# Routing attention: the centroid products moved behind the sums of weights, with the choice, the codes, the division and the row writes moved after them

## The chip, the cores and the metric

The kernel runs on one core of a Trainium2 chip. The metric is the device time of one execution in microseconds (us). Three runs of the kernel before took 707.80, 705.94 and 705.63 us, with a median of 705.94. A profile records one execution, instruction by instruction, with the engines PE (TensorE: matmuls), DVE (VectorE), ACT (ScalarE), POOL (GpSimd) and SP (SyncE, which here only issues DMAs).

## The reference

Two blocks follow each other. The first is attention in which a query sees only keys of its own cluster; the second sends each token to one of eight experts.

```python
# attention: B=4, H=8, S=768, D=64, 16 clusters a head
q_assign = np.argmax(np.einsum('bhsd,hcd->bhsc', q_n, c_n), axis=-1)   # q, k, centroids divided
k_assign = np.argmax(np.einsum('bhsd,hcd->bhsc', k_n, c_n), axis=-1)   # by their norms
mask = q_assign[:, :, :, None] == k_assign[:, :, None, :]
scores = np.where(mask, scale * np.matmul(q, k.transpose(0, 1, 3, 2)), -1000000000.0)
attn = np.exp(scores - np.max(scores, axis=-1, keepdims=True))
attn = attn / (np.sum(attn, axis=-1, keepdims=True) + 1e-09)
x = np.matmul(attn, v)            # then (B,H,S,D) -> (B*S, H*D) = (3072, 512)
# experts: E=8, 512 -> 1024 -> 512
expert_idx = np.argmax(xn @ en.T / tau, axis=1)
out[mask] = gate_w[mask, None] * (np.maximum(x[mask] @ w1[e], 0.0) @ w2[e])
```

## The kernel before

Attention goes by pairs of heads: 16 pairs (`n`), four to a batch (`nb` = 0 to 3 in batch `b`). A pair has twelve units, that is two halves of the queries times six blocks of 128 keys, and is worked in six turns (`it` = 0 to 5) of two units each. In a turn the code writes, in this order: the scores and the exponents of the two units that come next (so turn 5 computes scores of the next pair), then `between(n, it)`, then `attend` for this turn's two units, then some work that is named by the turn. Every engine runs its instructions in the order in which this code writes them; nothing reorders them later.

A unit's scores (L484) are four short matmuls on `hot` (bf16), which add a large negative number where clusters differ, and four float matmuls of queries and keys, all on quarters of the array (64*64). ACT takes the exponent (`expo`, L495) into one of five buffers `prob`. `attend` multiplies with the values (L506, 64*64 as well), and DVE adds the exponents up in `acc` (L515 for the first two units of a half, L525 for the others). At the end of a half (turns 2 and 5), ACT copies the result out (`o_sb`, L530) and POOL joins its two parts (`unite`, L539).

The mask of the next pair is prepared during a pair, in steps:
- `turn0` and `turn1` (L386) turn the queries and keys of the pair after next, on DVE, in turns 4 and 5.
- `products` (L396): PE multiplies queries and keys with the centroids, on column strips of the array (128*32), into a bank of `misc`; DVE brings it out (`asn`, L405). Turn 0, ahead of `attend`.
- `choose`: four DVE operations (L414 to L417) find the chosen cluster; three ACT operations (L419, L422) write the codes `cd`; then SP issues a transposing DMA (L427) that makes `hot` of them. Turn 1.
- `hot` is first used by the scores of turn 5.

The result of the pair before is finished in the same pair:
- `total`: PE sums `acc` over the keys (L553, 128*32, into a bank of `misc`), DVE turns the sums and inverts them (L570, L571), POOL spreads the inverses (L574). Turn 0, after `attend`.
- `divide`: DVE makes `den` (L585) and `xT` (L589). Turn 2, after `attend`.
- `rows`: DVE turns `xT` into rows `xb` (L606) and SP writes them to `x_rows` with four DMAs (L613). Turn 3.

There are two `misc` banks, handed out in turn. In the first pair of each later batch the products for the routing of the batch before (L632, 128*32) stand in turn 4; from pair 10 on, small hooks for the early experts (`ranks`, L768, `firsts`, `dest`, `hot_rows`, `tokens`, L950) are put between the turns. SP's other DMAs come from the same code: v of the next pair in turn 2 (L195), q and k of a later pair in turns 4 and 5 (L208), reads of `x_rows` (L654) and, from pair 11, expert weights (L1091). After the last pair the experts' stage takes the rest of the time; it is not touched.

Of the kernel before, what the change touches and what calls it, by code (L numbers as in the profile page):

```python
# [39 lines left out]
def kernel(  # L40
# [140 lines left out]
    NP = len(pairs)  # L181
# [43 lines left out]
    def keep_up(n):  # L225

        for _ in range(n):
            nc.tensor.matmul(
                idle_ps[:, 0].rearrange("p (g x) -> p g x", x=P),
                lhsT=onesb,  # L230
                rhs=bc(onesb, [P, 4, P], 1),
                start=True,
                stop=True,
            )
# [88 lines left out]
    def begin():  # L323

        nc.scalar.dma_start(out=c_sb, in_=centroids.rearrange("h c d -> (h c) d"))
        load(0, "q")
        load(0, "k")
        load(0, "v")
        load(1, "qk")
        constants()  # L330

        nc.scalar.activation(en_r, epsc[0:E], ACTF.Sqrt)
        nc.scalar.dma_start(out=emb, in_=moe_expert_emb)
        nc.scalar.dma_start(out=tau, in_=moe_tau.to_broadcast([E, 1]))
        norm_rows(cn_r, c_sb, P)
        unit_centroids()
        keep_up(2)
        piece(0, "turn0")
        piece(0, "turn1")
        norm_rows(en_r, emb, E)  # L340

        nc.scalar.activation(cn_r, epsc, ACTF.Exp)
        piece(0, "products")
        for m in range(2):
            scores(m, (1,))
        piece(0, "choose")
        keep_up(6)
        piece(0, "turn_numbers")
        for m in range(2):
            scores(m, (0,))  # L350
            expo(m)
        token_numbers()
        unit_experts()

    def prep_pieces(n):

        hp = pairs[n][1]
        t = ld[n]

        def in_halves(kT):  # L360

            return kT.rearrange("p (s i t) -> p i s t", i=2, t=SQ)

        def turn(nm, half):
            if half == 0:
                t[nm + "T"] = trp.tile([P, S], F32, tag=nm + "T", name=nm + "T")
            bk = misc()
            for j in range(NJ // 2):
                nc.tensor.transpose(
                    bk[:, P * j : P * j + P],  # L370
                    t[nm][:, NJ // 2 * half + j].rearrange("p h d -> p (h d)"),
                    ident,
                )
            if nm == "q":
                nc.scalar.copy(t["qT"][:, HS * half : HS * half + HS], bk[:, 0:HS])
            else:
                nc.vector.tensor_copy(
                    in_halves(t["kT"])[:, half], bk[:, 0:HS].rearrange("p (s t) -> p s t", t=SQ)
                )

        def turn_blocks(nm):
            t[nm + "T"] = trp.tile([P, S], F32, tag=nm + "T", name=nm + "T")
            dst, src = t[nm + "T"], t[nm].rearrange("p j h d -> p (j h d)")
            if nm == "k":
                dst, src = in_halves(dst), src.rearrange("p (i s t) -> p i s t", i=2, t=SQ)
            nc.vector.transpose(dst, src)  # L386

        def products():

            bk = misc()  # L390
            for i in range(4):
                if i < 2:
                    r = t["qT"][:, HS * i : HS * i + HS]
                else:
                    r = in_halves(t["kT"])[:, i - 2]
                nc.tensor.matmul(  # L396
                    bk[2 * C * i : 2 * C * i + 2 * C, 0:HS],
                    lhsT=cnB[:, hp],
                    rhs=r,
                    start=True,  # L400
                    stop=True,
                )

            t["asn"] = smp.tile([P, HS], F32, tag="asn", name="asn", bufs=1)
            nc.vector.transpose(t["asn"], bk[:, 0:HS])  # L405

        def choose():

            shp = [P, S // SQ, C]
            asn = t["asn"].rearrange("p (g c) -> p g c", c=C)  # L410
            amax = smp.tile(shp[0:2], F32, tag="amax", name="amax")
            sel = smp.tile(shp, BF16, tag="sel", name="sel", bufs=1)
            pm = smp.tile(shp[0:2], BF16, tag="pm", name="pm")
            nc.vector.tensor_reduce(amax, asn, axis=AXX, op=ALU.max)  # L414
            nc.vector.tensor_tensor(sel, asn, bc(amax, shp, 2), ALU.is_equal)
            nc.vector.tensor_tensor(sel, sel, bc(prefc, shp, 1), ALU.mult)
            nc.vector.tensor_reduce(pm, sel, axis=AXX, op=ALU.max)  # L417
            pm = pm.rearrange("p (s h) -> p s h", h=2)
            nc.scalar.activation(cd[..., 1], pm, ACTF.Copy, scale=wcd)  # L419
            for i, p0 in enumerate((0, D)):  # L420
                g = slice(p0, p0 + D)
                nc.scalar.activation(  # L422
                    cd[g, :, :, 2 * i], pm[g], ACTF.Square, scale=(BIG**0.5, 1.0)[i]
                )
            t["H"] = trp.tile([P, S // (2 * SQ), P], BF16, tag="hot", name="hot")
            if n > 0:
                nc.sync.dma_start_transpose(  # L427
                    out=t["H"], in_=cd.rearrange("p s h c -> p (s h c)")
                )

        def turn_numbers():

            U = S // (4 * SQ)
            for half in range(2):
                bk = misc().bitcast(BF16)
                for u in range(U):
                    nc.tensor.transpose(
                        bk[:, P * u : P * u + P],
                        cd[:, U * half + u].rearrange("p h c -> p (h c)"),
                        identb,  # L440
                    )
                bk = bk[:, 0 : P * U].rearrange("r (s x) -> r s x", x=P)
                ss = slice(U * half, U * half + U)
                nc.scalar.copy(t["H"][:, ss, D:], bk[:, :, D:])
                nc.vector.tensor_copy(t["H"][:, ss, 0:D], bk[:, :, 0:D])

        return {
            "turn0": lambda: turn_blocks("q") if n else (turn("q", 0), turn("k", 0)),
            "turn1": lambda: turn_blocks("k") if n else (turn("q", 1), turn("k", 1)),
            "products": products,  # L450
            "choose": choose,
            "turn_numbers": turn_numbers,
        }

# [840 lines left out]
    prepare, route = {}, {}  # L1295
# [30 lines left out]
    def piece(n, name, *args):  # L1326
        if n < NP:
            if n not in prepare:
                prepare[n] = prep_pieces(n)
            prepare[n][name](*args)  # L1330

    def between(n, it):
        b, nb = divmod(n, NHP)
        if n == 0:

            if it == 0:
                piece(1, "turn0")
                piece(1, "turn1")
            elif it == 1:
                piece(1, "products")  # L1340
            elif it == 2:
                piece(1, "choose")
                turned_experts()
            elif it == 3:
                later_constants()
        elif it == 0:
            piece(n + 1, "products")
        elif it == 1:
            piece(n + 1, "choose")
        elif it == 3:  # L1350
            rows(2 * n - 2, 2 * n - 1)
        if it == 4:
            piece(n + 2, "turn0")
# [2 lines left out]
        if b > 0:  # L1356
            if nb == 0 and it == 3:
                route[b - 1] = route_pieces(b - 1)
            products, logits, read, norms, choose = route.get(b - 1, (None,) * 5)


            m = NJ * nb + it
            if m in (8, 11, 14):
                read((m - 8) // 3 * 2, (m - 8) // 3 * 2 + 2)
            if m in (15, 16, 18, 19, 21, 22):
                norms((15, 16, 18, 19, 21, 22).index(m))
            if (nb, it) == (0, 4):
                products(0, 1)
            elif (nb, it) == (0, 5):
                logits(0, 1)  # L1370
            elif (nb, it) == (1, 4):
                choose()
# [29 lines left out]
    with tc.manual_schedule(engines=by_hand):  # L1402
        begin()
        for i in range(0, len(units), 2):
# [8 lines left out]
            for m in range(i + 2, min(i + 4, len(units))):  # L1413
                scores(m)
                expo(m)
            between(n, it)
            if it == 4 and n == NP - 1:
                divide(2 * n)
# [8 lines left out]
            for m in range(i, i + 2):  # L1427
                attend(m)
            if it == 2:
                if n > 0:  # L1430
                    divide(2 * n - 2, 2 * n - 1)
                unite(2 * n)
            elif it == 5:
                unite(2 * n + 1)
            if i + 2 == len(units):
# [1 line left out]
                route[b][0](0)  # L1437
            if it == 0 and n > 0:
                total(2 * n - 2, 2 * n - 1)
            elif it == 3 and n == NP - 1:  # L1440
                total(2 * n)
        at.close()
        mop = ctx.enter_context(tc.tile_pool(name="mop", bufs=2, **tile_waits))
# [196 lines left out]
```

## Time and profile before

| what | value |
|---|---|
| median of three runs | 705.94 us |
| the profiled execution: its own time | 709.17 us |
| its span, first to last instruction | 707.4 us |
| granted TensorE clock, mean | 0.996 |
| PE busy | 692.3 us |
| DVE busy | 382.0 us |
| ACT busy | 264.5 us |
| POOL busy | 263.0 us |
| scores on `hot` (L484), 768 matmuls | 65.5 us, 329 ns each |
| float scores (L484), 1536 matmuls | 156.8 us, 484 ns each |
| values' products (L506), 1536 matmuls | 142.0 us, 486 ns each |
| centroid products (L396), 128 matmuls | 498 ns each |
| sums of weights (L553), 248 matmuls | 15.9 us, 338 ns each |
| exponents (L495), 192 | 153.5 us, 811 ns each |

A float matmul stands as two instructions, and the four quarters or strips of the array work at once, so the means are not a rate. Matmuls are pipelined and their ends are modelled; the start of an instruction is the surer number. In the lines below, "x8" means that eight instructions of one kind are shown as one, the first number is the start in us from the span's start, and a bracket gives the engine's idle time before it and what ended it. Waits of SP are not shown as idle time.

### The profile page before, as it was taken

How to read it: one execution, taken by the hardware profiler on the slowest of the kernel's cores; microseconds unless marked ns; L12 is line 12 of the kernel's file. 1: busy time of each engine (PE TensorE's matmuls, PEld its weight loads, DVE VectorE, ACT ScalarE, POOL GpSimd, SP SyncE). 2: the span in 40 equal slices, each digit the busy share in tenths (PEclk: the TensorE clock that was granted, in tenths of full speed). 3: DMA queues.
4: the chain of work that ended last, by engine and by line, in shares of the span. 5: the costliest groups of instructions: out<-in, count | busy, mean ns of one | idle time of the engine just before them, and what ended most of it. 6: DMA issues, size and time to landing. Idle time of an engine off the chain costs nothing.

```text
span 707.4 us, 16123 instructions
## 1 busy us (share of the span) xinstructions
PE 692.3 (98%) x6518; PEld 455.4 (64%) x6518; DVE 382.0 (54%) x665; ACT 264.5 (37%) x446; POOL 263.0 (37%) x402
## 2 busy tenths in 40 slices
PE   7999999999999999999999999999999999999997
PEld 3444444444444444454966668897979797979694
DVE  4688888998889999998583121240220303030310
ACT  4566655577566655676315110101010111111111
POOL 2122221322224221454224446656264454635403
PEclk9999999999999999999999999999999999999999
DMA  9546656776657787779799977268758486869360
GB/s 148 84 65 105 105 99 100 139 158 114 100 92 158 125 147 157 158 188 331 172 317 347 333 281 271 71 241 288 258 211 305 183 312 220 313 228 341 123 247 31
DMA packets 244123, 135.54 MB, mean 192 GB/s; under 512 B 207808, under 2 KB 207810, under 8 KB 244044
## 3 DMA queue, kind: packets, MB, share of 16 engines
q1 hardware_dynamic: 237852, 121.28, 63.8%
q0 software_dynamic: 6016, 13.12, 5.3%
q8 instruction: 54, 0.88, 0.5%
q14 instruction: 25, 0.20, 0.1%
q10 hardware_dynamic: 176, 0.05, 0.0%
HBM read 115.92 MB, written 13.12 MB: 182 GB/s over the span
## 4 chain that ended last, share of the span: by engine, by line
PE 80%; DVE 6%; issue 5%; DMA 5%; another core or an unknown queue 1%; ACT 1%; POOL 1%; SPq 1%; POOLq 0%; DVEq 0%; ACTq 0%
PE s_ps L484 19%; PE o_ps L506 15%; PE h_ps L1261 10%; PE y_ps L1277 9%; PE h_ps L1176 9%; PE y_ps L1213 5%; PE misc L1213 5%; PE x_ps L1176 3%; DMA out_dram<-ys,spidx 3%; DVE acc L525 2%; PE misc L553 2%; PE misc L396 2%; DMA x_rows<-xb 1%; PE misc L632 1%
## 5 line engine op out<-in xcount | busy, mean ns | idle before, releaser
L495 ACT ACTIVATE prob<-s_ps 128x768 f32<-128x768 f32 x192 | 153.5, 811 | 97.1 <-PE s_ps L484 83.4
L484 PE MATMUL s_ps<-qT,kT 64*64 64x384 f32 x1536 | 156.8, 484 | 0.0
L506 PE MATMUL o_ps<-prob,v 64*64 64x385 f32 x1536 | 142.0, 486 | 0.0
L525 DVE TENSOR_TENSOR acc<-acc,prob 128x768 f32<-128x768 f32 x128 | 125.7, 982 | 8.8 <-ACT cd L422 0.5
L506 PEld LDWEIGHTS o_ps<-prob,v 64*64 64x64 f32 x1536 | 54.7, 133 | 70.2 <-issue 58.4
L1222 DVE STREAM_TRANSPOSE ys<-y_ps 128x256 f32<-128x256 f32 (+4 forms) x16 | 6.6, 414 | 155.4 <-PE y_ps L1213 138.7
L1261 PE MATMUL h_ps<-xTm,w1s 128*128 128x128 f32 x768 | 88.6, 275 | 1.4 <-issue 1.4
L1261 PEld LDWEIGHTS h_ps<-xTm,w1s 128*128 128x128 f32 x768 | 87.6, 192 | 3.0 <-issue 2.6
L1277 PE MATMUL y_ps<-w2s,hT 128*128 128x512 f32 x192 | 85.3, 594 | 1.7 <-ACT hT L1268 1.0
L539 POOL TENSOR_TENSOR o_sum<-o_sb 128x385 f32<-128x385 f32 x30 | 31.4, 1048 | 148.1 <-ACT o_sb L530 148.1
L1052 POOL DMA_INDIRECT out_dram<-ys,spidx x56 | 56.9, 1017 | 74.1 <-DVE ys L1236 59.4
L484 PEld LDWEIGHTS s_ps<-qT,kT 64*64 64x64 f32 x1536 | 56.4, 134 | 38.5 <-issue 35.3
L1268 ACT ACTIVATE hT<-h_ps 128x512 f32<-128x512 f32 x24 | 14.3, 596 | 162.9 <-PE h_ps L1261 119.1
L1176 PE MATMUL h_ps<-xTs,w1s 128*128 128x272 f32 (+7 forms) x384 | 72.9, 346 | 1.1 <-ACTq L1537 1.1
L1176 PEld LDWEIGHTS h_ps<-xTs,w1s 128*128 128x128 f32 x384 | 66.6, 190 | 8.0 <-issue 2.4
L484 PE MATMUL s_ps<-hot 64*64 64x384 bf16 x768 | 65.5, 329 | 2.4 <-ACT prob L495 1.3
L574 POOL COPY inv<-inv 32x12 f32<-32x12 f32 x120 | 42.9, 358 | 55.2 <-DVE inv L571 50.8
L1277 PEld LDWEIGHTS y_ps<-w2s,hT 128*128 128x128 f32 x192 | 35.3, 190 | 42.9 <-issue 40.2
L1041 POOL DMA_INDIRECT xs<-x_rows,gpidx x56 | 56.4, 1007 | 17.1 <-issue 16.5
L484 PEld LDWEIGHTS <-hot 64*64 64x64 bf16 x768 | 23.7, 107 | 40.3 <-issue 39.1
L1213 PE MATMUL y_ps<-hTs,w2o 128*128 128x272 f32 (+7 forms) x256 | 48.0, 346 | 0.0
L1213 PE MATMUL misc<-hTs,w2o 128*128 128x272 f32 (+7 forms) x256 | 48.0, 346 | 0.0
(264 smaller groups left out, 680.0 us busy)
## 6 DMA issues: line engine op xcount, KB each, us to landing
w1s<-in_moe_w_dram SPq DMA_DIRECT2D x18, 2048.0 KB
w2s<-in_moe_w_dram SPq DMA_DIRECT2D x18, 2048.0 KB
v<-in_v_dram SPq DMA_DIRECT2D x128, 48.0 KB
q<-in_q_dram SPq DMA_DIRECT2D x60, 96.0 KB
k<-in_k_dram SPq DMA_DIRECT2D x60, 96.0 KB
x_rows<-xb SPq DMA_DIRECT2D x60, 96.0 KB
xr<-x_rows SPq DMA_DIRECT2D x9, 512.0 KB
w1s<-in_moe_w_dram SPq DMA_DIRECT2D x4, 1024.0 KB
```

Source lines behind the costliest of these rows:

```text
L484: nc.tensor.matmul(s_ps[D * half : D * half + D, h, 0:HS], lhsT=l[rows, half], rhs=r[rows], start=part == (1 if len(parts) < 2 else 0), st ...
L495: nc.scalar.activation(d["prob"][:, :, 0:HS], d["s_ps"][:, :, 0:HS], ACTF.Exp, scale=scale)
L506: nc.tensor.matmul(g["o_ps"][D * h : D * h + D, half, 0:HE], lhsT=ld[n]["v"][keys, j, h], rhs=d["prob"][keys, h, 0:HE], start=(j == 0), st ...
L525: nc.vector.tensor_tensor(g["acc"], g["acc"], d["prob"][:, :, 0:HS], ALU.add)
L539: add(t["o_sum"][:, hq], t["o_sb"][:, 0], t["o_sb"][:, 1], ALU.add)
L574: nc.gpsimd.tensor_copy(inv2[M * to : M * to + M, :, i % 2], inv[M * i : M * i + M])
L1041: nc.gpsimd.indirect_dma_start(out=to, out_offset=None, in_=of, in_offset=bass.IndirectOffsetOnAxis(ap=at, axis=0), bounds_check=n - 1, oo ...
L1052: inst = nc.gpsimd.indirect_dma_start(out=to, out_offset=bass.IndirectOffsetOnAxis(ap=at, axis=0), in_=of, in_offset=None, bounds_check=n - 1,
L1176: nc.tensor.matmul(bk, lhsT=w1s[it.slot][:, c, P * f : P * f + P], rhs=d["xT"][:, c, 0:C], start=(c == 0), stop=(c == KD - 1),)
L1213: nc.tensor.matmul(bks[g][:, 0:C], lhsT=d["w2"][:, f, P * g : P * g + P], rhs=d["hT"][:, f, 0:C], start=(f == 0), stop=(f == KF - 1),)
L1261: nc.tensor.matmul(bk[:, m : m + P], lhsT=w1s[it.slot][:, c, f0 + m : f0 + m + P], rhs=d["xT"][:, P * c : P * c + P], start=(c == 0), stop ...
L1277: nc.tensor.matmul(bk, lhsT=d["hT"][:, P * c : P * c + P], rhs=w2s[it.slot][:, c], start=(c == 0), stop=(c == KF - 1),)
```

## The change

Six pieces of work are written at other places:
- `products` goes from ahead of `attend` in turn 0 to behind `total`, which is behind `attend`. (In pair 0, which has no `total`, it stays in turn 1 but goes behind `attend`.)
- `choose` goes from turn 1 to turn 2. It is cut in two: its ACT operations and the transposing DMA become `codes`, which ACT runs in turn 3, between the exponents of that turn's two units.
- `divide` goes from turn 2 to turn 3.
- `rows` goes from turn 3 to turn 0 of the following pair; the last ones are written in turn 4 of pair 15.
- The routing products of a finished batch stay in turn 4 but go behind `attend`.

No operation is added or left out.

```diff
@@ -344,6 +344,7 @@
         for m in range(2):
             scores(m, (1,))
         piece(0, "choose")
+        piece(0, "codes")
         keep_up(6)
         piece(0, "turn_numbers")
         for m in range(2):
@@ -415,7 +416,10 @@
             nc.vector.tensor_tensor(sel, asn, bc(amax, shp, 2), ALU.is_equal)
             nc.vector.tensor_tensor(sel, sel, bc(prefc, shp, 1), ALU.mult)
             nc.vector.tensor_reduce(pm, sel, axis=AXX, op=ALU.max)
-            pm = pm.rearrange("p (s h) -> p s h", h=2)
+            t["pm"] = pm.rearrange("p (s h) -> p s h", h=2)
+
+        def codes():
+            pm = t["pm"]
             nc.scalar.activation(cd[..., 1], pm, ACTF.Copy, scale=wcd)
             for i, p0 in enumerate((0, D)):
                 g = slice(p0, p0 + D)
@@ -449,6 +453,7 @@
             "turn1": lambda: turn_blocks("k") if n else (turn("q", 1), turn("k", 1)),
             "products": products,
             "choose": choose,
+            "codes": codes,
             "turn_numbers": turn_numbers,
         }
 
@@ -1336,18 +1341,16 @@
             if it == 0:
                 piece(1, "turn0")
                 piece(1, "turn1")
-            elif it == 1:
-                piece(1, "products")
             elif it == 2:
                 piece(1, "choose")
                 turned_experts()
             elif it == 3:
                 later_constants()
-        elif it == 0:
-            piece(n + 1, "products")
-        elif it == 1:
+        elif it == 0 and n > 1:
+            rows(2 * n - 4, 2 * n - 3)
+        elif it == 2:
             piece(n + 1, "choose")
-        elif it == 3:
+        elif it == 4 and n == NP - 1:
             rows(2 * n - 2, 2 * n - 1)
         if it == 4:
             piece(n + 2, "turn0")
@@ -1364,9 +1367,7 @@
                 read((m - 8) // 3 * 2, (m - 8) // 3 * 2 + 2)
             if m in (15, 16, 18, 19, 21, 22):
                 norms((15, 16, 18, 19, 21, 22).index(m))
-            if (nb, it) == (0, 4):
-                products(0, 1)
-            elif (nb, it) == (0, 5):
+            if (nb, it) == (0, 5):
                 logits(0, 1)
             elif (nb, it) == (1, 4):
                 choose()
@@ -1413,6 +1414,8 @@
             for m in range(i + 2, min(i + 4, len(units))):
                 scores(m)
                 expo(m)
+                if it == 3 and m == i + 2:
+                    piece(n + 1, "codes")
             between(n, it)
             if it == 4 and n == NP - 1:
                 divide(2 * n)
@@ -1427,9 +1430,9 @@
             for m in range(i, i + 2):
                 attend(m)
             if it == 2:
-                if n > 0:
-                    divide(2 * n - 2, 2 * n - 1)
                 unite(2 * n)
+            elif it == 3 and n > 0:
+                divide(2 * n - 2, 2 * n - 1)
             elif it == 5:
                 unite(2 * n + 1)
             if i + 2 == len(units):
@@ -1437,7 +1440,11 @@
                 route[b][0](0)
             if it == 0 and n > 0:
                 total(2 * n - 2, 2 * n - 1)
-            elif it == 3 and n == NP - 1:
+            if it == (0 if n else 1):
+                piece(n + 1, "products")
+            if (nb, it) == (0, 4) and b > 0:
+                route[b - 1][0](0, 1)
+            if it == 3 and n == NP - 1:
                 total(2 * n)
         at.close()
         mop = ctx.enter_context(tc.tile_pool(name="mop", bufs=2, **tile_waits))
```

## The prediction

> **What bounds the kernel now.** I read the page first: the span, the busy shares and the summed chain.
>
> ```profile
> span 707.4 us, 16123 instructions
> PE 692.3 (98%) x6518; PEld 455.4 (64%) x6518; DVE 382.0 (54%) x665; ACT 264.5 (37%) x446; POOL 263.0 (37%) x402
> ```
>
> TensorE has work nearly all the time and makes up 80% of the chain. The change touches only the attention stage (about 15 to 340 us), where the chain in order of time is PE piece after PE piece. There, time is won only by taking something off PE and lost only where PE is made to wait. So I went to PE's instructions in order of time: first pair 0, where the centroid products (L396) stand alone between scores and values' products, then a usual pair, which has sums of weights (L553) too.
>
> ```profile
> 22.25 0.84 PE L484 MATMUL s_ps<-qT,kT 64*64 64x384 f32 x8
> 23.02 0.52 PE L396 MATMUL misc<-qT,cnB 128*32 128x384 f32 x2
> 23.80 1.52 PE L506 MATMUL o_ps<-prob,v 64*64 64x385 f32 x16
> 25.14 0.34 PE L484 MATMUL s_ps<-hot 64*64 64x384 bf16 x4
> ...
> 77.01 0.81 PE L484 MATMUL s_ps<-qT,kT 64*64 64x384 f32 x8
> 77.75 0.52 PE L396 MATMUL misc<-qT,cnB 128*32 128x384 f32 x2
> 78.54 1.52 PE L506 MATMUL o_ps<-prob,v 64*64 64x385 f32 x16
> 79.99 0.88 PE L553 MATMUL misc<-acc,ones 128*32 128x192 f32 x16
> 80.80 0.36 PE L484 MATMUL s_ps<-hot 64*64 64x384 bf16 x4
> ```
>
> Starts are what counts here, since ends are modelled. A turn without either block starts its next scores 0.65 + 1.29 = 1.94 us after its last float scores (170.06 less 169.42, then 171.35 less 170.06). With L396 alone it is 25.14 - 22.25 = 2.89: the block costs 0.95. With both it is 80.80 - 77.01 = 3.79: they cost 1.85 together. Each streams for 0.65 (as long as the scores' float part, with the same columns; L553 has half of them, twice over). So a visit to the 128*32 form costs about 0.28 beyond its streaming: 0.10 going in (0.74 for 0.65), 0.14 coming out (0.79 for 0.65), the rest in the matmuls after it.
>
> Next I read what ACT, SP and PE do around the codes and the transfer of `hot`, which the next pair's first scores need:
>
> ```profile
> 160.78 1.62 ACT L495 ACTIVATE prob<-s_ps 128x768 f32<-128x768 f32 x2 [2.56 <-PE s_ps L484]
> 162.73 0.40 ACT L419 ACTIVATE cd<-pm,wcd 128x24 bf16<-128x24 bf16 x1 [0.33 <-DVE pm L417]
> 162.95 0.61 ACT L422 ACTIVATE cd<-pm 64x24 bf16<-64x24 bf16 x2
> 166.59 1.62 ACT L495 ACTIVATE prob<-s_ps 128x768 f32<-128x768 f32 x2
> ...
> 163.59 1.40 SPq L427 DMA_TRANSPOSE hot<-cd  x1
> 165.11 4.97 SPq L195 DMA_DIRECT2D v<-in_v_dram  x8
> ...
> 165.54 0.33 PE L484 MATMUL s_ps<-hot 64*64 64x384 bf16 x4
> 171.35 0.33 PE L484 MATMUL s_ps<-hot 64*64 64x384 bf16 x4
> ```
>
> 165.54 starts turn 3 of that pair, 171.35 turn 5, whose scores are the next pair's and need `hot`. The transfer was issued at 163.59. The semaphore times recorded in the trace give its last completion at 166.85, 3.26 later. Over the 15 pairs that time is 3.20 to 3.42 for twelve, with median 3.27; the others are 3.89, 4.41 and 3.23 (with one late completion). Nothing was moving when it started:
>
> ```profile
> 163.50:164.70 1.20, 1.20 (x24) 0.64 (x20) 1.06 (x2) 1.18 (x4) 0.30 (x2) 1.00 0.00 0
> 164.70:165.20 0.50, 0.50 (x12) 0.15 (x8) 0.43 (x1) 0.50 (x2) 0.00 (x0) 1.00 0.92 214
> ```
>
> (The last two numbers are DMA share and GB/s.) So `hot` now lands 4.5 us before its use: a long cover.
>
> **The change, part by part.**
>
> *Products behind the sums (PE).* For pairs 1 to 14 the two 128*32 blocks become neighbours: one visit instead of two, 0.28 saved. Nothing else is saved, as every matmul stays. Bound below: 0, if two 128*32 blocks with different weights also pay at their seam; route products (L632) pay nothing between their rounds (1.44 for 4 rounds of 0.32, and one exit), so I take the full saving. In pair 10 `ranks` (L768) stays in front of the values' products and keeps its own visit: 0.1. In pairs 10 and 11 DVE is late: their successors' sums take 1.41 and 1.47 us instead of 0.88, waiting for `acc` (L525), and what PE saves there is waited away. That leaves 12 pairs: 12 x 0.28 = 3.4 us. In pair 0 the block changes sides of L506: 0. The route products (turn 4 of the first pair of a batch, L632) do the same: 0; their xT, now divided a turn later, is ready about 1 us into turn 4 and used 2.9 us into it.
>
> *Choice, division, rows (DVE, SP, POOL).* No instruction is added. DVE's stream per pair loses one wait for PE (asn 0.73) and is spread more evenly. From the start of `sums` to the last `acc` that the next sums need, DVE now takes 16.28 us (140.58 to 156.86), and PE asks 18.31 after that start (158.89). Rows leave this stretch (-0.91) and asn enters it (+0.51): 15.9. PE asks after 19.05 - 0.97 = 18.1, 0.97 being the way from L553 to `sums`. That leaves 2.2, so sums do not become a new wait in usual pairs. Rows (0.91) now stand behind the last `acc`, ahead of nothing that PE needs at once. POOL's copies (L574, 3.07) have until turn 3 instead of 2. On SP the four x_rows writes move ahead of v, v ahead of `hot`: rows ready 2 us into turn 0, writes 2.3 to 3.8, v 4 to 5: v is issued by about 10 us of the pair, landed by 11.5, and `hot` comes at 12.9. So the queue is empty again. The exception is an x_rows read (0.44 to issue, L654) that follows v in turn 2 of 6 pairs, and POOL's gathers in pair 14: together 0.6 us, an estimate from the one transfer at 3.89 (0.6 over the usual). In pair 14 PE waits 0.38 for an exponent held by `acc` (L515), now ahead of the division: 0.4 gained. In pair 15 DVE's work moves about 1 us later; the route products at 334.74 ask for an xT that I reckon at 334.4: covered, barely.
>
> *Codes and `hot` (ACT, SP).* This is the price. Let X be the start of turn 3. The first exponent starts at X + 1.05 (166.59), held by PE and the copy before it. The next ACT instruction can start 0.70 later, as a norm does after the pair's second exponent (167.40 to 168.11). The three codes take 0.83 (162.73 to 163.56). So they end at X + 2.58, the issue follows 0.03 later (163.56, 163.59), and landing 3.27 after that: X + 5.88. PE wants `hot` at X + 5.81 (171.35 - 165.54), its weights 0.3 sooner. A landing reaches PE some 0.14 late (k's at 6.87, L369 at 7.00). So PE waits 5.88 + 0.14 - 5.81 = 0.2 us per pair. Bounds: 0 if it hides, 0.83 with the slow transfer of 3.89. I take 0.2, because twelve of fifteen transfers lie within 0.2 of each other. Thirteen pairs (0 to 9, 12 to 14): 13 x 0.2 = 2.6 us; in 10 and 11 it falls into DVE's lateness. The second exponent of turn 3 is pushed from X + 1.86 to X + 2.6 and ends at X + 3.4; PE needs its bank at X + 3.72: 0.3 of cover. The codes' wait for the choice (0.33) goes: pm is ready about 1.3 before X.
>
> [...]
>
> **Sum.** -3.4 - 0.1 - 0.4 + 2.6 + 0.6 = -0.7 us. The profiled execution (span 707.4, its own time 709.17) becomes 708.5; that execution stands 3.23 over the median 705.94, so for the median: 705.2.
>
> **Rivals.**
> A, `hot` is covered after all (its tail or my 0.14 is shorter): -3.4 - 0.1 - 0.4 = -3.9, 702.0. For it: the margin is 0.2 in 5.8. Against: even the shortest 3.20 gives 0.13.
> B, `hot` is later, and the kernel slower: break-even is at 0.25 per pair (3.3 / 13). At 0.5, where a transfer takes 3.57, it is 13 x 0.5 + 0.6 - 3.9 = +3.2: 709.1. For it: 3.89 and 4.41 occur with other transfers in flight, and q is now issued right behind `hot`. Against: v was issued right behind it before.
> C, the seam between sums and products costs what a switch costs: no 3.4, so +2.7: 708.6. Against: L632.
> D, DVE is the limit of a pair: PE's saving and `hot`'s lateness both vanish in waits of L553: 705.9. Against: 2.2 us of slack.
>
> **How the numbers follow.** Mine 0.42, A 0.22, B 0.22, C 0.08, D 0.06. I call 0.3% (2.1 us) what a measurement of this kernel can tell from no change: faster is below 703.8, slower above 708.1. Mine spans a wait of 0.1 to 0.3 per pair, 703.9 to 706.5: within, but for 0.05 on the fast side and 0.01 on the slow. A is faster but for 0.02. B is slower but for 0.03, C slower, D within. Faster 0.25, within 0.47, slower 0.28. The range goes from A with pairs 10 and 11 saving too (2 x 0.28 = 0.6: 701.4) to B at 0.56 per pair (13 x 0.56 + 0.6 - 3.9 = +4.0: 709.9) and leaves out at most 0.2, mostly B's longer waits; mine alone is 703.9 to 706.5.
>
> **What would show it.** Right: L396 directly behind L553 with about 1.5 us from L553 to the next scores; the idle time of weight loads or of L484 on `hot` with releaser DMA, about 0.2, once per pair; pairs 19.25 apart by their sums (19.33 before). Wrong: pairs of 19.05 (A), of 19.5 or more (B), a first start of L396 over 0.8 behind L553 (C), or L553 waiting for L525 in every pair (D).

## The result, and the profile after

The changed kernel is slower: its median over seven runs is 710.28 us, that of the kernel before over seven runs 705.94. The ratio is 1.0055, with a 95% interval from 1.0041 to 1.0069. The forecast was 705.2 within 701.4 to 709.9. The profiled execution took 713.0 us, 2.7 over the median, with a span of 711.1. From the page of the changed kernel, the span, the busy shares and the summed chain:

```profile
span 711.1 us, 16104 instructions
PE 692.0 (97%) x6518; PEld 460.4 (65%) x6518; DVE 383.8 (54%) x665; ACT 264.4 (37%) x446; POOL 270.6 (38%) x402
PE 78%; DMA 9%; issue 6%; DVE 4%; ACT 1%; POOL 1%; POOLq 0%; SPq 0%; DVEq 0%; ACTq 0%
```

The summed chain of the kernel before, from its page:

```profile
PE 80%; DVE 6%; issue 5%; DMA 5%; another core or an unknown queue 1%; ACT 1%; POOL 1%; SPq 1%; POOLq 0%; DVEq 0%; ACTq 0%
```

PE's busy time is the same, its share of the chain is lower, and DMA has gone from 5% to 9%. The waits of the changed kernel, engine and line, what was waited for, us in total, times, and the longest, say which DMA:

```profile
PE s_ps L489 <- DMA hot<-cd: 4.3, 7, 2.1
PE misc L558 <- DVE acc L530: 1.4, 2, 0.9
...
PEld L489 <- DMA hot<-cd: 12.7, 13, 2.8
```

The kernel before has no wait for this DMA. Here the first scores of a pair (L489, L484 before) wait for it, and their weight loads, which run ahead, 13 times. PE's instructions in order of time show both what was won and what was lost, in pair 2:

```profile
72.97 1.46 PE L511 MATMUL o_ps<-prob,v 64*64 64x385 f32 x16
74.63 0.36 PE L489 MATMUL s_ps<-hot 64*64 64x384 bf16 x4 [0.19 <-DMA hot<-cd]
...
79.17 1.46 PE L511 MATMUL o_ps<-prob,v 64*64 64x385 f32 x16
80.57 0.88 PE L558 MATMUL misc<-acc,ones 128*32 128x192 f32 x16
81.24 0.50 PE L397 MATMUL misc<-qT,cnB 128*32 128x384 f32 x2
...
82.02 0.36 PE L489 MATMUL s_ps<-hot 64*64 64x384 bf16 x4
```

Won: the centroid products (L397) start 0.67 us behind the sums (L558), and the next scores 0.78 behind that, 1.45 from L558 to the scores as forecast. Lost: the scores on `hot` start 74.63 - 72.97 = 1.66 us behind the values' products, where 1.30 is the way without a wait: 0.36 late. What ACT and SP did for that pair (turn 3 starts at X = 68.45):

```profile
69.50 0.81 ACT L500 ACTIVATE prob<-s_ps 128x768 f32<-128x768 f32 x1
70.34 0.40 ACT L423 ACTIVATE cd<-pm,wcd 128x24 bf16<-128x24 bf16 x1
70.56 0.62 ACT L426 ACTIVATE cd<-pm 64x24 bf16<-64x24 bf16 x2
...
71.21 1.42 SPq L431 DMA_TRANSPOSE hot<-cd  x1
```

The codes start at X + 1.89, `hot` is issued at X + 2.76 and lands at X + 6.13, and PE wanted it at X + 5.82. In pair 6 the same transfer took 5.32 us instead of 3.38. The first group below is what moved during pair 2's transfer, the second what moved during pair 6's (queue: packets, MB, share of the 16 engines):

```profile
q1 hardware_dynamic: 2245, 0.48, 66.6%
...
q1 hardware_dynamic: 2952, 0.87, 111.7%
q8 instruction: 1, 0.02, 2.0%
```

In the second stands a packet of an instruction queue, a load of code; the experiments come back to it. What the long wait of pair 6 did to PE, first its instructions and then its granted clock (the number before the last two; 1.00 is the full clock):

```profile
152.10 1.46 PE L511 MATMUL o_ps<-prob,v 64*64 64x385 f32 x16
155.70 0.36 PE L489 MATMUL s_ps<-hot 64*64 64x384 bf16 x4 [2.13 <-DMA hot<-cd]
...
156.70 1.44 PE L489 MATMUL s_ps<-qT,kT 64*64 64x384 f32 x8
157.91 2.58 PE L511 MATMUL o_ps<-prob,v 64*64 64x385 f32 x16
```

```profile
155.60:156.60 1.00, 0.90 (x16) 0.50 (x20) 1.00 (x2) 0.00 (x0) 0.00 (x0) 1.00 1.50 161
156.60:157.60 1.00, 1.00 (x16) 0.51 (x12) 0.90 (x2) 0.81 (x1) 0.00 (x0) 0.58 1.56 142
157.60:158.60 1.00, 1.00 (x12) 0.29 (x8) 1.00 (x2) 0.40 (x1) 0.00 (x0) 0.50 1.61 137
158.60:159.60 1.00, 1.00 (x12) 0.45 (x8) 0.97 (x2) 0.41 (x1) 0.00 (x0) 0.50 1.59 135
159.60:160.60 1.00, 1.00 (x16) 0.44 (x12) 0.41 (x1) 0.00 (x0) 0.00 (x0) 0.72 1.60 143
```

PE stood 2.30 us (155.70 - 152.10 - 1.30), and a microsecond later its clock was at half for 3.4 us, which cost another 1.68 us on the scores and the values' products (the four rows lack 1.70 us of full clock). That was in this execution; a second profile below has the wait without the dip.

### The profile page after: what moved, and what is told of

Read it like the earlier page. It is cut to its first block, busy times and chain, and to the rows that moved or that the text cites. A ratio compares the mean times of both kernels' runs of the same rounds, so it can differ in the third digit from the quotient of the medians.

```text
span 711.1 us, 16104 instructions
## 1 busy us (share of the span) xinstructions
PE 692.0 (97%) x6518; PEld 460.4 (65%) x6518; DVE 383.8 (54%) x665; ACT 264.4 (37%) x446; POOL 270.6 (38%) x402
## 4 chain that ended last, share of the span: by engine, by line
PE 78%; DMA 9%; issue 6%; DVE 4%; ACT 1%; POOL 1%; POOLq 0%; SPq 0%; DVEq 0%; ACTq 0%
PE s_ps L489 18%; PE o_ps L511 13%; PE h_ps L1266 10%; PE y_ps L1282 10%; PE h_ps L1181 9%; PE misc L1218 5%; PE y_ps L1218 5%; DMA hot<-cd 5%; DMA out_dram<-ys,spidx 3%; PE x_ps L1181 3%; PE misc L558 2%; PE misc L397 2%; DVE acc L530 1%; PE misc L637 1%; DMA k<-in_k_dram 1%
## 5 line engine op out<-in xcount | busy, mean ns | idle before, releaser
L489 PE MATMUL s_ps<-qT,kT 64*64 64x384 f32 x1536 | 157.7, 487 | 0.0
L511 PEld LDWEIGHTS o_ps<-prob,v 64*64 64x64 f32 x1536 | 58.9, 134 | 65.8 <-issue 59.5
L489 PEld LDWEIGHTS s_ps<-qT,kT 64*64 64x64 f32 x1536 | 55.7, 134 | 34.3 <-issue 30.2
L489 PE MATMUL s_ps<-hot 64*64 64x384 bf16 x768 | 65.1, 329 | 6.7 <-DMA hot<-cd 4.3
L579 POOL COPY inv<-inv 32x12 f32<-32x12 f32 x120 | 47.9, 399 | 49.1 <-DVE inv L576 44.8
L489 PEld LDWEIGHTS <-hot 64*64 64x64 bf16 x768 | 24.2, 107 | 56.2 <-issue 41.8
```

The costliest lines, as they stand in the source:

```text
L489: nc.tensor.matmul(s_ps[D * half : D * half + D, h, 0:HS], lhsT=l[rows, half], rhs=r[rows], start=part == (1 if len(parts) < 2 else 0), st ...
L511: nc.tensor.matmul(g["o_ps"][D * h : D * h + D, half, 0:HE], lhsT=ld[n]["v"][keys, j, h], rhs=d["prob"][keys, h, 0:HE], start=(j == 0), st ...
L579: nc.gpsimd.tensor_copy(inv2[M * to : M * to + M, :, i % 2], inv[M * i : M * i + M])
```

## The experiments

Four theories were held against each other. **1**: the loss is PE's wait for `hot`, because the codes stand too late on ACT. **2**: the division's new place on DVE costs. **3**: the rows' earlier place, with its DMAs, costs. **4** came up after the first four runs: the slow transfers of `hot` are caused by loads of code. Four kernels at a time ran side by side on one chip; ratios are to the kernel before on that chip, with their 95% intervals. The times in the first four expectations are on the scale of the first result, where the kernel before took 705.94 us; on the chip of those four runs it took 703.34, so they are to be compared by the ratio.

### The codes first in turn 3 (e1_codes_first)

```diff
+            if it == 3:
+                piece(n + 1, "codes")
             for m in range(i + 2, min(i + 4, len(units))):
                 scores(m)
                 expo(m)
-                if it == 3 and m == i + 2:
-                    piece(n + 1, "codes")
```

> The changed kernel with one edit: in turn 3 the three codes stand ahead of both exponents on ACT, no longer between them. Theory 1 (the whole loss is that `hot` is issued too late in turn 3): the codes no longer wait for the first exponent (start about X + 1.0 instead of X + 1.89, X being the start of turn 3), the issue comes at X + 1.9, landing 3.35 later at X + 5.3, ahead of PE's X + 5.8; PE waits for `hot` only where a transfer takes over 3.9 us (the 4.12, 5.32 and 4.85 of the changed kernel). The loss of 4.3 us becomes a gain of 2 to 4: 702 to 704. Bound: the codes may push the first exponent by up to 0.8, if they are not ready to run before X + 1.05; then the values' products of that turn are late and 13 x 0.3 = 4 us come back: 707. Theory 2 (the division and acc order on DVE) and theory 3 (the rows' earlier place on SP and POOL): this edit touches neither, 709 to 711.

Measured: 706.86 us, ratio 1.0044 (1.0031 to 1.0057), which is 709.0 on the first scale: theory 1's 702 to 704 was missed. `hot` was issued 0.75 us earlier (X + 2.0), and nine pairs did not wait. But the other six had transfers of 4.1 to 4.9 us (three of them, 7, 10 and 13, had been quick), and these alone gave 3.7 us of waiting, as much as PE saves. So the place of the codes is part of the cause, and the slow transfers, which I had taken for a few outliers, are another. The ratio alone would hide this: of the 3.8 us by which this span (705.6) exceeds that of the kernel before in its second profile below (701.8), 2.3 stand ahead of the attention stage of the table below, where the clock was at half from 15.8 to 22.7 us, and only 1.0 in it.

### The products alone (e3_products_alone)

From the kernel before; choice, codes, division and rows stay where they were.

```diff
-        elif it == 0:
-            piece(n + 1, "products")
...
+            if it == (0 if n else 1):
+                piece(n + 1, "products")
```

> The kernel before with one part of the change: the centroid products directly behind the sums of weights, both behind the values' products; choice, codes, division and rows stay in their old turns (the choice in turn 1, `hot` issued in turn 1). Theory 1: PE's visits are saved and `hot` stays 3 us or more early: -3.4 to -3.9 us, 702.0 to 702.6. If the products' later place holds up the choice and with it DVE's other work of turn 1, up to 13 x 0.2 comes back: 704.6. Rival C of the prediction (the seam costs as a switch): 705.9, no change.

Measured: 703.35 us, ratio 0.9993 (0.9984 to 1.0003), which is 705.4 on the first scale, short of theory 1's gain. PE's merged visits are there (usual pairs 19.03 us apart instead of 19.32), and no scores wait for `hot`. But the sums now wait for `acc` in four pairs, where the kernel before waits in two:

```profile
135.79 0.51 PE L553 MATMUL misc<-acc,ones 128*32 128x192 f32 x2
136.48 0.55 PE L553 MATMUL misc<-acc,ones 128*32 128x192 f32 x8 [0.17 <-DVE acc L525]
```

That is turn 0 of pair 6, with pair 5's sums: 0.68 us late, and so are pair 13's; those of pairs 10 and 11 wait 1.45 and 1.40 instead of 0.53 and 0.59. In all the sums wait 4.2 us instead of 1.1, and most of the saving is waited away on DVE. About 0.9 us of it is left in the attention stage (309.27 us against 310.15, in the table below).

### Division and rows back (e5_rows_back), and the codes alone (e6_codes_alone)

The first is the changed kernel with `divide` in turn 2 and `rows` in turn 3 again. The second is the kernel before with only the codes moved.

```diff
-        elif it == 0 and n > 1:
-            rows(2 * n - 4, 2 * n - 3)
...
+        elif it == 3:
             rows(2 * n - 2, 2 * n - 1)
...
+                if n > 0:
+                    divide(2 * n - 2, 2 * n - 1)
                 unite(2 * n)
-            elif it == 3 and n > 0:
-                divide(2 * n - 2, 2 * n - 1)
```

> The changed kernel with the division back in turn 2 and the rows back in turn 3, codes left where the change put them. Theory 1: the wait for `hot` stays, 0.3 to 0.5 us per usual pair: 709 to 711.5. Theory 2 (the division's place on DVE): 706 or less. Theory 3 (the four x_rows writes ahead of v and `hot` in the queues, and the x_rows read beside `hot`): the slow transfers (5.32 and 4.85 us) become 3.3 to 3.5, which is worth about 2 + 1.5 + 1.7 us with the dip of the clock that followed: 705 to 707.

Measured: 706.62 us, ratio 1.0056 (1.0034 to 1.0078), which is 709.9 on the first scale, as theory 1 said. Theories 2 and 3 fall as the main cause. Quiet transfers are a little shorter (3.18 to 3.27 us, not 3.2 to 3.5), and pair 6 is quick, but pairs 12, 13 and 14 now take 4.83, 4.79 and 4.26 (the first two with a load of code inside, the third beside POOL's gathers), and `hot` is waited for 6.1 us in all.

```diff
...
             for m in range(i + 2, min(i + 4, len(units))):
                 scores(m)
                 expo(m)
+                if it == 3 and m == i + 2:
+                    piece(n + 1, "codes")
```

> The kernel before with one part of the change: the codes, and with them the issue of `hot`, between the two exponents of turn 3 instead of behind the choice in turn 1. Nothing is saved on PE. Theory 1: 13 pairs wait 0.3 to 0.5 us, and one or two slow transfers add 1 to 3 us: 710.5 to 714. If `hot` here costs nothing (theory 2 or 3): 706.

Measured: 710.91 us, ratio 1.0105 (1.0090 to 1.0119), which is 713.4 on the first scale, as theory 1 said. `hot` is waited for 6.3 us in all, and PE saves nothing: the pure price of this move.

### The codes in turn 2 (e2_codes_turn2, e7_turn2_rows_back)

```diff
...
         elif it == 2:
             piece(n + 1, "choose")
+            piece(n + 1, "codes")
...
-                if it == 3 and m == i + 2:
-                    piece(n + 1, "codes")
```

> The changed kernel with one edit: the codes stand directly behind the choice in turn 2, behind that turn's exponents, so `hot` is issued before turn 3 starts. Theory 1 (the loss is PE's wait for `hot`, with `hot` issued late and a slow transfer now and then): issue at about X - 0.5, landing at X + 2.8, or X + 4.4 where the transfer takes 4.9, all ahead of PE's X + 5.8: no pair waits. What stays is the 3.4 to 3.9 us off PE less the waits of the sums for DVE in pairs 10, 11 and 14 (some 1.0 more than before): -1.0 to -2.9 us against the kernel before, ratio 0.996 to 0.9985. Theories 2 and 3 (the new places of the division and of the rows cost by themselves): at or above the kernel before, ratio 1.000 to 1.003.

Measured: 703.64 us, ratio 0.9988 (0.9974 to 1.0001), just above what theory 1 gave (0.996 to 0.9985), with an interval that reaches into it. In most pairs `hot` is issued at X + 0.5 to 0.65 (later than I had put it, as the exponents of turn 2 end later), and although transfers of up to 4.98 us occur, no pair waits: the first scores of pair 2's successor come 1.29 us behind the values' products.

```profile
71.53 1.46 PE L511 MATMUL o_ps<-prob,v 64*64 64x385 f32 x16
72.82 0.33 PE L489 MATMUL s_ps<-hot 64*64 64x384 bf16 x4
```

The sums wait 3.6 us for `acc` (those of pairs 5, 9, 10, 11 and 13), so again DVE takes back most of what PE saves. With the division and the rows moved back as well:

> The changed kernel with the codes in turn 2 and, besides, the division back in turn 2 and the rows back in turn 3. Theory 1: within 0.5 us of the run with the codes in turn 2 alone, as the places of division and rows only matter to a `hot` that has no time to spare. Theories 2 and 3: 1 to 3 us faster than that run.

Measured: 704.10 us, ratio 0.9995 (0.9984 to 1.0007), within 0.5 us of the run before, as theory 1 said. So with `hot` early, the places of division and rows do not matter much; what the changed kernel loses, it loses through `codes`.

### Both kernels again (a0_after_again, e0_before_again)

> The changed kernel itself, to be set beside the others of this call and to see whether its slow transfers are chance. In its first profile `hot` took 4.12 us in pair 0, 5.32 in pair 6 and 4.85 in pair 12, each with a load of code (a packet of the instruction queues) starting 1 to 3 us after the issue; transfers without one took 3.2 to 3.5. If loads of code are the cause, they stand at the same place of the program in each execution: the same pairs are slow again (0, 6, 12 at 4 to 5.3; 5 and 13 at 3.4 to 3.6), and the ratio is 1.005 to 1.006 again. If it is chance, other pairs are slow.

Measured: 708.18 us, ratio 1.0051 (1.0032 to 1.0070). The slow transfers are not chance: pair 0 took 3.98 us, pair 6 4.82, pair 12 4.91, and pairs 5 and 13 3.73 and 3.91, each with a load of code again; pair 6 without the dip of the clock.

> The kernel before, for a profile on this chip in the same call. The first profile of it had a clock of 0.50 from 16 to 19 us, ahead of the first pair, and lay 3.2 us over the median. An execution without that dip should stand at 1.5 to 1.7 us less, with the pairs 19.32 apart as before and `hot` slow in pairs 1 and 8 again (4.4 and 3.9), hidden.

Measured: 703.65 us, a span of 701.8. No dip ahead of the first pair, usual pairs 19.32 apart, pairs 1 and 8 at 3.75 and 3.84 us, hidden. For the attention stage, from turn 3 of pair 0 to the last sums, every wait can be read off PE's starts (us). Before, changed and codes in turn 2 ran on one chip, the other four on another; what follows the stage, which no edit touches, took 363.9 to 364.4 us in all seven profiles, so they can be set against each other:

| kernel | stage | waits for `hot` | sums for `acc`, scores for ACT | left: saved by the merged visits |
|---|---|---|---|---|
| before (again) | 310.15 | 0 | 2.07 | |
| changed (again) | 313.77 | 6.48 | 3.17 | -3.96 |
| codes first | 311.14 | 3.65 | 3.35 | -3.94 |
| codes in turn 2 | 308.65 | 0 | 4.35 | -3.78 |
| products alone | 309.27 | 0 | 5.05 | -3.86 |
| division and rows back | 313.11 | 6.05 | 2.85 | -3.87 |
| codes alone | 315.99 | 6.26 | 1.34 | +0.31 |

The last column is the stage less that of before, less the change of both kinds of waits. It is the same -3.8 to -4.0 wherever the blocks are merged, and about nothing where they are not, so the account closes.

### Moving the loads of code (e8_code_shift)

```diff
-        keep_up(9)
+        for _ in range(61):
+            nc.tensor.matmul(
+                idle_ps[:, 0, 0 : P // 2],
+                lhsT=onesb,
+                rhs=onesb[:, 0 : P // 2],
+                start=True,
+                stop=True,
+            )
```

> The changed kernel with PE's program made 104 instructions longer ahead of the first pair: the 9 idle matmuls of the start, 512 columns each, become 61 of 64 columns (each is a weight load and a matmul). In the profiles so far 16 KB of PE's program are loaded per 256 of its weight loads and matmuls, so every load of code moves 104 of them, about 3.7 us, ahead of the same place of the work. Theory 4 (what makes `hot` slow is a load of code that starts 0 to 2 us, or 2.5 to 3, behind its issue): by the times of the loads in the profiles of the changed kernel the slow pairs move. Pairs 2, 3, 9 and 10 get a load 0.6 to 1.5 us behind the issue and wait 0.8 to 1.6 us each (they waited 0.2 to 0.5); pairs 5, 6 and 13 get none and wait 0.2 to 0.4 (they waited 0.5 to 2.3). Pair 0, whose load is another queue's, stays at about 1.0. The time stays within 2 us of the changed kernel's: ratio 1.003 to 1.009. If the slow transfers come from what the pairs themselves move (the x_rows read of pair 6, the gathers of late pairs), pairs 6, 12 and 13 stay slow and 2, 3, 9 and 10 quick.

Measured: ratio 1.0104 (1.0070 to 1.0137). What moved during the transfers of pairs 1 and 12, first in the changed kernel (pair 1 took 3.34 us, pair 12 4.85):

```profile
q1 hardware_dynamic: 2190, 0.47, 66.5%
...
q1 hardware_dynamic: 1678, 0.84, 70.3%
q8 instruction: 1, 0.02, 1.2%
```

and then with the longer program (pair 1 took 4.91, pair 12 3.28):

```profile
q1 hardware_dynamic: 3124, 0.59, 60.5%
q8 instruction: 1, 0.02, 1.3%
...
q1 hardware_dynamic: 1587, 0.47, 69.9%
```

The slow transfers went where the loads went: pairs 1, 2 and 9 took 4.91, 5.03 and 5.00 us and waited 1.9 to 2.0 each, while pairs 5 and 12 fell to 3.28. My list was half wrong, because the loads moved 2.1 to 2.5 us and not 3.7: they now stood 2.8 to 3.0 behind the issue in pairs 1, 2 and 9, the worst place, and 0.1 to 0.3 behind it in pairs 3, 4 and 10. The waits for `hot` add up to some 11 us, against 6.5 in the changed kernel, and that is why the kernel got slower than expected. Pair 6 lost its load and still took 4.11: it has an x_rows read beside it, issued 1.5 us ahead of `hot`. That much of the other explanation is true. Pair 0, whose load comes from another queue, stayed at 4.08 us.

### The codes last (e4_codes_last)

```diff
                 expo(m)
-                if it == 3 and m == i + 2:
-                    piece(n + 1, "codes")
+            if it == 3:
+                piece(n + 1, "codes")
```

> The changed kernel with one edit: the codes stand behind both exponents of turn 3, 0.8 us later. Theory 1: issue at X + 3.55, landing at X + 6.8 (a transfer of 3.25), so PE waits 1.0 us for `hot` where it waited 0.2 to 0.3; pairs 4 and 8 have 1.5 us more cover and wait 0. 11 pairs x 0.8 = 9 us more, less or more by a few us as other pairs meet a load of code, and up to 2 x 1.7 us where the wait passes 2 us and the clock falls: ratio to the kernel before 1.015 to 1.023 (the changed kernel had 1.005). Theories 2 and 3: 1.005.

Measured: ratio 1.0187 (1.0153 to 1.0221), as theory 1 said. Pairs without a load of code wait 0.8 to 1.2 us. The waits for `hot` add up to 18 us, 4.7 of them in pair 14, where POOL's gathers ran beside a transfer of 6.9 us and the clock stood at 0.50 for over 6 us.

### The idle matmuls of the start (e9_turn2_warm, e10_before_warm)

The profiles differed by up to 3 us before the attention stage had begun: in eight of the twelve above the clock fell to 0.50 at 15.8 to 17.5 us, for 3.4 or 6.8 us. The first of these kernels has the codes in turn 2, the second is the kernel before; both get:

```diff
-        keep_up(6)
+        keep_up(10)
         piece(0, "turn_numbers")
+        keep_up(4)
```

> The kernel with the codes in turn 2 (ratio 0.9988), and besides more idle matmuls in two gaps of PE ahead of the first pair: 10 instead of 6 between the first scores and the turning of the codes, and 4 behind that. In about half of all executions, of the kernel before too, the clock was at 0.50 for 3 to 4 us at 16 to 20 us, which costs 1.5 to 1.7 us. Theory (the gaps of 1.0 us at 13.0 and 14.9 us let the clock fall): the dip is gone in nearly all executions, and the median falls to the 702.2 us of those that had none: ratio 0.997 to 0.998. If the gap of 1.5 us at 16.1 us alone decides, nothing changes: 0.9988.

Measured: 707.68 us, ratio 0.9955 (0.9932 to 0.9979).

> The kernel before with the same idle matmuls more, as the counterpart: what the idle matmuls are worth without any part of the change. If they remove the dip at 16 to 20 us: the executions stand at the 703.2 us of those without it, ratio 0.9985 to 0.9995, and 1.0 us above the kernel with the codes in turn 2 and the same matmuls. If not: 1.000.

Measured: 709.15 us, ratio 0.9991 (0.9976 to 1.0006). The kernel before took 710.21 on this chip, with a spread from 707.0 to 716.7; the two with more idle matmuls spread less (706.0 to 710.1 and 708.4 to 710.2). The clock ahead of the first pair, with the codes in turn 2 (first two lines) and with the idle matmuls besides (last two):

```profile
17.00:19.00 2.00, 1.82 (x16) 1.02 (x19) 2.00 (x3) 0.83 (x2) 0.00 (x0) 0.50 1.43 153
19.00:21.00 2.00, 2.00 (x20) 0.96 (x19) 1.90 (x3) 1.17 (x2) 0.00 (x0) 0.64 0.48 66
```

```profile
17.00:19.00 2.00, 1.85 (x28) 1.21 (x31) 2.00 (x3) 1.59 (x3) 0.00 (x0) 1.00 1.47 159
19.00:21.00 2.00, 2.00 (x32) 1.10 (x28) 1.90 (x3) 0.83 (x2) 0.00 (x0) 1.00 0.48 66
```

So e9_turn2_warm is a version that beats the kernel before, and by the ratios the changed one too, beside which it did not run: the merged visits, the codes early enough, and a start without the dip. By the medians, 707.68 against 709.15, about 1.5 us of it is the part of the merged visits; the rest, 1.1 us, is the start, which by itself is not clear of the noise (0.9976 to 1.0006).

## Why the prediction was wrong

- **Products behind the sums**: right. I put 0.28 on a visit. With 0.1 for pair 10 that is 13 x 0.28 + 0.1 = 3.7 over pairs 1 to 14 before any wait, and the account, which sets waits apart, gives 3.8 to 4.0 in each kernel with merged visits. The seam is no switch (rival C falls).
- **Pairs 10 and 11**: right that they win nothing, but mis-sized. Around them sums and scores wait 1.1 us more than before, which eats more than their part of the saving; the sum of the prediction had about -0.1 for such waits (0.3 for pair 11's lost saving less 0.4 gained in pair 14). That is 1.2 us of the miss.
- **Choice, division, rows**: right for the changed kernel, as no usual pair waits for `acc`. But the slack of 2.2 us was read in one usual pair. For the sums of pairs 5 and 13 it is not there: once `hot` is early, they wait about 0.6 us each. Both are second pairs of a batch, where the routing's `choose()` of the batch before has its place (the hook at (1, 4) in the diff); that this is the work that makes DVE late is argued, not shown. So rival D holds in some pairs, and with pairs 10 and 11 it is why moving the codes back earns only 0.1% (0.9988).
- **Codes and `hot`, the usual pair**: right in size. The codes start at X + 1.89 in most pairs, 0.13 later than I reckoned, and PE starts 0.04 behind the landing, not 0.14. In the pairs without a load of code, 4 and 8 left out, the wait is 0.24 us in the mean, in both profiles; I had said 0.2. The thirteen pairs were not the right ones: 4 and 8 do not wait at all, because in the first pair of a batch the route products, now behind `attend`, come ahead of those scores and give 1.5 us more cover, while pairs 10 and 11 do wait (0.30 and 0.02 us in the first profile).
- **Collisions**: this is the step that failed. I priced the slow transfers at 0.6 us "in all", for an x_rows read and POOL's gathers. In the changed kernel the five pairs with a load of code behind the issue (0, 5, 6, 12, 13) wait 4.4 and 4.6 us in the two profiles, against 1.2 if they had been usual: 3.3 us more, and 1.7 for the dip of the clock in the first. About 0.8 of it, in pair 6, may be the x_rows read: in e8_code_shift the transfer took 4.11 us there without a load, against the usual 3.27. The trace of the kernel before had it: its transfers of 4.41 and 3.89 us, in pairs 1 and 8, had a packet of an instruction queue inside them, the 3.26 one in pair 7 had none. The DMA engines in 40 slices of the transfer (each digit is their busy share in tenths) and the packet, first in pair 1, then the engines in pair 7:

```profile
DMA  0000000005069999900000000699999999999355
q8 instruction: 1, 0.02, 1.4%
...
DMA  0000000000000017999999999999999931466412
```

  In pair 1 they stand for eight slices, 0.9 us, in the middle of the transfer. The prediction's 3.23 "with one late completion", in pair 14, is a third: its last completion came 4.83 us behind the issue, with a load of code starting 2.56 behind it, and PE needs all sixteen. I took 12 like durations out of 15 as the rule and priced the rest as exceptions, without asking what they had in common. With 3 us of cover they cost nothing; with none they cost what they take.

The sum of the second profiles: -3.96 for the visits, +6.48 for `hot`, +1.10 for DVE's and ACT's lateness, +3.6 in all, where I had -0.7. Of the 4.3 us between, 3.3 are in `hot` (I had 2.6 + 0.6) and 1.2 in DVE and ACT, less 0.2 that the visits gave beyond my sum. That is nearly rival B, whose number of 709.1 stood for 0.5 us per pair (6.48 over 13 pairs is 0.5); its reason, transfers beside other transfers, was only a part of the truth.

## What to carry to other kernels

A DMA that lands just in time has no usual duration: count its slow cases as they are, not their median, and look in the trace for what each slow one shares. Here that was a load of code, which stood at a fixed place of the program, so the same pairs lost in both profiles of the changed kernel, and an edit of PE's program ahead of them moved the loss elsewhere. And when PE's work per pair shrinks, look at the next engine in every pair that carries extra work, not in a usual one: two of sixteen took back a third of the gain.

## What the hardware showed that was not expected

**A load of code delays a transposing DMA.** The profile counts 54 packets on q8 of 16 KB each, for 13,036 weight loads and matmuls of PE, one per about 240; lengthening PE's program moved them (and not those of q14). Over the 14 profiles there are 210 transfers of `hot`, sorted here by when a load started behind their issue:

| load of code starts | transfers | time to land, us |
|---|---|---|
| none while it runs | 135 | median 3.27; 123 up to 3.45 |
| q8, 0 to 0.45 us behind the issue | 17 | 3.36 to 3.91 |
| q8, 0.45 to 2.1 us | 12 | 3.71 to 5.32, more the later it starts |
| q8, 2.1 to 3.2 us | 27 | 9 at 3.2 to 3.45, 3 at 3.65 to 3.9, 15 at 4.7 to 5.0 |
| another instruction queue (q14, 8 KB) | 19 | 3.18 to 4.13, median 3.88 |

Of the 12 slower ones without a load, eight stood beside an x_rows read or POOL's gathers. In the fourth row often only the last of the transfer's 16 completions is late (in pair 12 of the changed kernel's first profile 4.85, the one before it 3.28). Why some escape, and how a load holds the transfer up, was not tried. The Trainium skill, "Runtime: NRT & Kernel Launch" (Instruction fetch mechanics), says that code comes in blocks of 16 KiB, 256 instructions, by a DMA queue of the engine's own, and that the cost is mostly hidden. The size and the spacing of q8's packets agree with it; q14's are half that size. For PE itself no wait for a load shows in its starts here; the DMA beside the loads is delayed.

**The clock falls after a shorter gap than thought.** PE stood 2.30 us in pair 6 and the clock then fell to 0.50 for 3.4 us; in the other profiles waits of 1.8 to 2.01 us were followed by no dip, one of 4.67 by a longer one. At the start several gaps of 0.6 to 1.1 us, 13 to 17 us into the span, were enough in eight profiles and not in four, and with two of them filled neither profile has the dip. The Trainium skill, "TensorE: Matmul & The Clock Gate" (Why this matters for your kernels), warns of idle gaps of more than about 3 us; in this kernel shorter ones did it, so a little filling is worth its few instructions.

What the clock records show beside this: each of the ten dips ahead of the last sums lasts 3.41 us or twice that, and the two of the changed kernel's first profile start 16.80 and 156.75 us into the span, 41 times 3.41 apart. So in these profiles the clock seems to be judged in fixed stretches of 3.41 us, and the idle time in one stretch adds up. PE was busy for 0.37 to 0.49 of the stretch ahead of each dip (1.27 of 3.41 us ahead of pair 6's), and in every other stretch at full clock of these profiles, from the first dip to the last sums, for at least 0.46. That this share decides is read from these records and was not tried. The stretch ahead of pair 6's dip and the dip:

```profile
153.34:156.75 3.41, 1.27 (x24) 0.63 (x24) 3.31 (x5) 0.56 (x2) 0.00 (x0) 1.00 1.12 172
156.75:160.16 3.41, 3.41 (x28) 1.31 (x24) 3.12 (x4) 1.62 (x2) 0.00 (x0) 0.50 1.60 139
```
